# Smaller alternating loads, norm sums on VectorE and spread scaling, in place of interleaved filter rows, in a spectral mixer on one core

## The chip, the cores and the metric

The kernel runs on one core of a Trainium2 chip. Its time is the device time in microseconds of one execution; the median of 3 runs is quoted, with lowest and highest. A profiled execution gives the span from the first to the last instruction, and the time of that execution is some 2 us longer than its span. Five engines work side by side and wait for each other by semaphores: TensorE (PE; its weight loads are listed as PEld), VectorE (DVE), ScalarE (ACT), GpSimd (POOL) and SyncE (SP), which here only issues transfers. Each engine works through its own instructions strictly in the order in which they were written.

## The reference

One input x of 2048 rows (S) by 512 columns (D), bf16, goes through two blocks with residuals:

```python
h  = x + irfft2( rfft2(layernorm(x)) * (w_r + 1j*w_i) )      # w_r, w_i: 2048 x 257
h2 = h + mixer(layernorm(h))

def mixer(x):                    # token mixing: along S, for each column d
    n = layernorm(x)
    u = gelu(einsum("sd,sf->df", n, w1) + b1)                # w1: 2048 x 1376
    y = einsum("df,fs->ds", u, w2) + b2                      # w2: 1376 x 2048
    return y.T
```

The layer norms are over D and have no scale or shift; the gelu is the tanh form.

## The kernel before

Row s of x is s = 16 p + i: partition p of 128, and i from 0 to 15. What has one i is called slice i here, 128 x 512; x and the result lie in SBUF as 16 such slices. Both Fourier transforms are matmuls with constant matrices, which are stored in the program and loaded (FP, EM and IF). The stages, by the names that the kernel's helpers give them:

- **ln1**: mean and variance of every slice, and from the variance the reciprocal root r. There are two ways: on VectorE a statistics instruction and an aggregate (L640, L642); or on ScalarE two passes with an accumulator, sum and sum of squares (L619), then two small POOL operations and one on VectorE (L631 to L635). The root is ScalarE's (L611), the reciprocal VectorE's (L613). The mean isn't subtracted from x here: it would change only frequency 0 of the transform along D, which is zero after a norm and which the kernel leaves out.
- **scaling** ("fs"): r is put not on x but on the transform matrix of the slice, FS = FP * r, 128 x 256 (L649), on VectorE or POOL.
- **f1**: the first part of the transform along S. For each slice four matmuls with 256 columns, two for each half b of the columns of x. Four slices make a quarter; a quarter and a half b fill two PSUM banks, which one instruction of ScalarE or VectorE evacuates into Y (128 x 1024).
- **f2**: the transform along D, in 16 units G of four matmuls with 256 columns and one evacuation of 128 x 512 into CS.
- **x** (u = 0 to 7): the rest of the transform along S, four matmuls with 512 columns from two units of f2 into two banks; then the *filter products* on VectorE, which read these banks, multiply them by the filter rows W (real part w = 0 and imaginary part w = 1) and write V (L701). These read PSUM directly, so both banks stay taken until the last product of this u.
- **g1** (u = 0 to 7): first part of the inverse, 16 matmuls with 128 columns from V, evacuated into PQ.
- **g2, g3** (slices): the rest of the inverse. Four matmuls with 256 columns, an evacuation into EO by ScalarE, three more matmuls, and a sum with x on VectorE, which gives h.
- **ln2**: the second norm of each slice of h, for which VectorE and ScalarE again share the sums; HH is h normed.
- **mm1, gelu, mm2**: the mixer's two products, 176 matmuls with 512 columns each, the gelu between them, and the final sum and store of each slice.

No order is written out by hand. Every instruction is handed to a builder class with its inputs and outputs, an engine, an assumed duration (`dur`) and a priority (`prio`). The method `schedule` then lists the instructions: of those whose inputs are there, the one that can start first by the assumed durations is next, priority decides among equals; a PSUM unit takes the banks that are free first, with a limit on how many units of a class may be open at once. The constant `LATENCY` is the assumed time from an engine's end to another's start, and a transfer's landing follows assumed rates. These numbers set the order and the banks and nothing else: the engines then wait by semaphores, in that order. Several readers of one unit's banks are chained, each waiting for the one before, also when both are on VectorE.

What the prediction's steps touch: the loads of x and FP, alternately on SP's and ScalarE's queue (X pieces of 2 or 4 slices, FP in two pieces); the list SUMS, by which slices 2, 3, 6, 7, 10, 11 and 15 have their sums on ScalarE; the choice of VectorE or POOL for each scaling; W, one tile in which the rows of both parts alternate, so that one product of 128 x 2048 serves u = 1 to 6 whole (u = 0 and u = 7 are cut into smaller ones); and the helpers `stage_f2`, `stage_x`, `stage_g1`, of which the last cuts the final evacuation (u = 7, par = 0) in two halves, one for ScalarE and one for VectorE.

Of the kernel before, what the change touches and what calls it, by code (L numbers as in the profile page):

```python
# [143 lines left out]
LATENCY = {"sp": 0.0, "pe": 230.0, "act": 130.0, "dve": 110.0, "pool": 80.0}  # L144
# [36 lines left out]
class Builder:  # L181
# [110 lines left out]
    def schedule(self):  # L292
# [12 lines left out]
        while len(order) < len(ops):  # L305
# [52 lines left out]
            if o.is_dma:  # L358
                eng_free[e] = st + 430.0
                x0 = max(st + 1300.0, dma_free)  # L360
                dma_free = x0 + o.bytes / (o.rate or (290.0 if x0 < 7000.0 else 400.0))
                o.finish = o.done = dma_free + 900.0
            else:
                o.done = st + (o.dur[e] if isinstance(o.dur, dict) else o.dur)
                o.finish = o.done + (LATENCY[e] if o.lat is None else o.lat)
                eng_free[e] = o.done
# [90 lines left out]
def memory_layout():  # L457
# [30 lines left out]
    add("W", [NP, NG, 2, 257], bf, rw)  # L488
    add("HH", [NP, NS2, D_LEN], bf, rw)
    rv = region(32768)  # L490
    add("V", [NP, NG, 2, 256], bf, rv)
# [26 lines left out]
def build_kernel(nc, A_x, A_w_r, A_w_i, B_w1, B_b1, B_w2, B_b2, out):  # L518
# [5 lines left out]
    K = Builder(nc, {"f1": 4, "f2": 2, "x": 2, "g1": 2, "g1t": 2, "g2": 2, "g3": 2, "mm1": 5, "mm1b": 6, "mm2": 8})  # L524
# [5 lines left out]
    W = T["W"]  # L530
# [20 lines left out]
    DUR = {"act": {256: 310.0, 512: 520.0, 1024: 960.0}, "dve": {256: 350.0, 512: 640.0, 1024: 1150.0}}  # L551

    def evac(name, engine, dst, srcf, unit, n, prio, last=True, outs=None):
        def emit(s, eng, bank):
            if s == "act":
                return eng.activation(dst, srcf(bank), ACT.Copy)  # L556
            return eng.tensor_copy(dst, srcf(bank))  # L557
        return K.op(name, engine, emit, outs=outs or [dst], dur=DUR[engine][n], unit=unit, pr=True, last=last, prio=prio)

# [4 lines left out]
    K.op("half", "pool", lambda s, eng, bank: eng.memset(T["mh"][:, 0:1], -0.5), outs=[T["mh"][:, 0:1]], dur=100.0, prio=20)  # L564
# [8 lines left out]
    ld_x(0, 2)  # L573
    ld_x(2, 4, "act")
    ld_x(4, 8)
    ld_fp(0, 8, "act")
    ld_x(8, 12)
    ld_x(12, 16, "act")
    ld_fp(8, 16)
    dma("ld_EM", EM[:], cin["EM"][:, :], 6656 * 128, outs=[EM[:]], prio=29)  # L580

    for g0, g1 in ((0, 4), (4, 16), (16, 32)):
        h0 = max(g0, 1)
        for w, dram in ((0, A_w_r), (1, A_w_i)):
            for comp in range(2):
                dma(f"ld_w{w}p{comp}_{g0}", W[comp:NP:4, g0:g1, w, :], bass.AP(dram.tensor, g0 * 257, [[64 * 257, 32], [257, g1 - g0], [1, 257]]),
                    32 * (g1 - g0) * 514, outs=[W[comp:NP:4, g0:g1, w, 0:240]], prio=28, rate=290.0)
                p0 = 2 + comp
                if g0 == 0:
                    dma(f"ld_w{w}z{comp}", W[p0:NP:4, 0:1, w, :], bass.AP(dram.tensor, 32 * 257, [[64 * 257, 32], [257, 1], [1, 257]]), 32 * 514,  # L590
                        outs=[W[p0:NP:4, 0:1, w, 0:240]], prio=28)
                dma(f"ld_w{w}m{comp}_{g0}", W[p0:NP:4, h0:g1, w, :],
                    bass.AP(dram.tensor, (64 - h0) * 257, [[64 * 257, 32], [-257, g1 - h0], [1, 257]]),
                    32 * (g1 - h0) * 514, outs=[W[p0:NP:4, h0:g1, w, 0:240]], prio=28, rate=290.0)
# [10 lines left out]

    mv, rs, sd = T["mv1"], T["rs1"], T["sd1"]
# [9 lines left out]
    def sums_act(name, src, func, bias, acc, k, prio):  # L616
# [3 lines left out]
             ins=[src] + ([bias] if bias is not None else []), outs=[jk, acc], dur=620.0, lat=320.0, prio=prio)  # L620

    SUMS = (2, 3, 6, 7, 10, 11, 15)
    for i0, i1 in ((0, 2), (2, 4), (4, 6), (6, 8), (8, 10), (10, 12), (12, 14), (14, 15), (15, 16)):
        sl = slice(i0, i1)
        sx, sq = T["sx1"][:, sl], T["sq1"][:, sl]
        mean, var, nb = mv[:, sl, 0], mv[:, sl, 1], T["nb1"][:, sl]
        if i0 in SUMS:
# [9 lines left out]
        else:  # L637
            for i in range(i0, i1):
                st = T["st1"][:, i, 0:6]
                K.op(f"ln1_st{i}", "dve", lambda s, eng, bank, st=st, i=i: eng.bn_stats(st, X[:, i, :]), ins=[X[:, i, :]], outs=[st],  # L640
                     dur=600.0, prio=20)
                K.op(f"ln1_ag{i}", "dve", lambda s, eng, bank, st=st, i=i: eng.bn_aggr(mv[:, i, :], st), ins=[st], outs=[mv[:, i, :]],  # L642
                     dur=110.0, prio=23)
        rstd(1, sl, var, EPS[:, 0:1], 1.0, 25)
        for i in range(i0, i1):
            r = rs[:, i:i + 1]
            eng_ = "pool" if i < 12 and i % 2 == 0 else "dve"
            K.op(f"fs{i}", eng_,
                 lambda s, eng, bank, i=i, r=r: eng.tensor_scalar(FS[:, i, :, :], FP[:, i, :, :], r, None, op0=ALU.mult),  # L649
                 ins=[FP[:, i, :, :], r], outs=[FS[:, i, :, :]], dur={"pool": 980.0, "dve": 210.0}[eng_], prio=26)  # L650
# [5 lines left out]
    for q in range(4):  # L656
        for b in range(2):
            unit = PsumUnit("f1", 2)
            for n in range(4):
                n2 = 4 * q + n  # L660
# [11 lines left out]
            def src(bank):  # L672
                v = ps[:, bank:bank + 2, :].rearrange("p b (h g k) -> p (b h) g k", h=2, k=4)
                return v.rearrange("p n g k -> p g n k")
            evac(f"f1_{q}_{b}_ev", "dve" if q >= 1 and b == 0 else "act", Yv[:, b, :, 4 * q:4 * q + 4, :], src, unit, 1024, 14)


    def stage_f2(G):
        for pars in ((0,), (1,)) if G == 0 else ((0, 1),):
            unit = PsumUnit("f2", 1)  # L680
            for par in pars:
                for b in range(2):
                    mm(f"f2_{G}_{par}{b}", lambda bank, par=par: ps[:, bank, par * 256:par * 256 + 256],
                       Y[:, b, par, 2 * G:2 * G + 2, :].rearrange("p g k -> p (g k)"), E[:, b, par, :],
                       unit, b == 0, b == 1, par == pars[0] and b == 0, 12 - 0.05 * G, 256)
            y = slice(pars[0], pars[-1] + 1)
            evac(f"f2_{G}_ev{pars[0]}", "dve" if pars[0] else "act", CS[:, G, :, :].rearrange("p c (y j) -> p y c j", y=2)[:, y],
                 lambda bank, y=y: ps[:, bank, :].rearrange("p (y c j) -> p y c j", y=2, c=2)[:, y], unit, 256 * len(pars), 10)


    def times_filter(name, unit, u, srcf, gs, last, ys=slice(0, 2), ws=slice(0, 2)):
        g0, gn, gk = gs
        gsl = slice(g0, g0 + (gn - 1) * gk + 1, gk)
        nw, ny = ws.stop - ws.start, ys.stop - ys.start

        def tt(s, eng, bank):
            src = srcf(bank)
            wv = W[:, gsl, ws, 1:257].rearrange("p g w (j y) -> p g w y j", y=2)[:, :, :, ys, :]
            ov = V[:, gsl, ws, :].rearrange("p g w (y j) -> p g w y j", y=2)[:, :, :, ys, :]
            src = bass.AP(src.tensor, src.offset, [list(src.ap[0]), [256, gn], [0, nw], [128, ny], [1, 128]])  # L700
            return eng.tensor_tensor(ov, src, wv, ALU.mult)  # L701
        K.op(name, "dve", tt, ins=[W[:, gsl, ws, 1:240]], outs=[V[:, gsl, ws, ys.start * 128:ys.stop * 128]],
             dur=gn * nw * ny * 128 / 0.96 + 75.0, unit=unit, pr=True, last=last, prio=11)

    def stage_x(u):
        if u == 0:
            for i in range(2):
                unit = PsumUnit("x", 1)
                for r in range(2):
                    for cs in range(2):  # L710
                        mm(f"x_{u}_{r}{cs}{i}", lambda bank, r=r: ps[:, bank, r * 256:r * 256 + 256],
                           M[:, 2 if i == 0 and r == 0 else r, cs, :], CS[:, i, cs, :], unit, r == 0 and cs == 0, cs == 1, r == 0 and cs == 0, 13, 256,
                           skip=True)
                for w in range(2):
                    times_filter(f"x_{u}_w{i}{w}", unit, u, lambda bank: ps[:, bank, :], (i, 2, 2), w == 1, ws=slice(w, w + 1))
            return
        unit = PsumUnit("x", 2)
        for r in range(2):
            for cs in range(2):
                mm(f"x_{u}_{r}{cs}", lambda bank, r=r: ps[:, bank + r, :], M[:, r, cs, :], CS[:, 2 * u:2 * u + 2, cs, :],  # L720
                   unit, cs == 0, cs == 1, r == 0 and cs == 0, 13, 512)
        gs = (4 * u, 4, 1)
        if u < 7:
            times_filter(f"x_{u}_w", unit, u, lambda bank: ps[:, bank, :], gs, True)
        else:
            times_filter(f"x_{u}_w1", unit, u, lambda bank: ps[:, bank, 128:256], gs, False, ys=slice(1, 2))
            for w in range(2):
                times_filter(f"x_{u}_w0{w}", unit, u, lambda bank: ps[:, bank, 0:128], gs, w == 1, ys=slice(0, 1), ws=slice(w, w + 1))


    def stage_g1(u):
        for par in (1, 0):
            split = u == 7 and par == 0
            for gs in ((0, 1), (2, 3)) if split else ((0, 1, 2, 3),):
                unit = PsumUnit("g1t" if split else "g1", 1, early=True)
                for w in range(2):
                    for gi in gs:
                        g = 4 * u + gi
                        mm(f"g1_{g}_{par}{w}", lambda bank, gi=gi: ps[:, bank, gi * NP:gi * NP + NP],
# [151 lines left out]
```

## Time and profile before

| | |
|---|---|
| median of 3 runs | 138.36 us (138.27 to 138.36) |
| profiled execution: span, time | 136.0 us, 138.27 us |
| TensorE matmuls busy | 120.6 us (89%), 747 recorded |
| VectorE busy | 79.2 us (58%), 165 |
| ScalarE busy | 64.6 us (47%), 141 |
| POOL busy | 18.0 us (13%), 49 |
| read from HBM, written | 20.54 MB, 2.10 MB |

The profile's page lists the busy time of each engine, the span in slices, the transfers, and the chain of work that ended last: from the last instruction back, at each step, to what released it. A share in this chain says more than a busy share: what isn't in the chain has slack. The matmuls' durations reach from a matmul's start to the modelled end of its pipeline, so consecutive ones overlap: a 128 x 512 one is listed with 379 ns, and 49 of them in a row take 10.74 us, 0.219 us each. VectorE's and ScalarE's neighbours can overlap a little too. In a group's line stand the operation, what it writes and reads, its count, busy time and mean duration, and the idle time before it with what ended that.

### The profile page before, as it was taken

To read this page: it belongs to the slowest core of one execution; us is meant where nothing else is said; L and a number is where in the kernel's file an instruction comes from. 1 tells how busy PE (TensorE), PEld (TensorE's weight loads), DVE (VectorE), ACT (ScalarE), POOL (GpSimd) and SP (SyncE) were. 2 spreads that over 40 slices of the span, in tenths; PEclk is the share of its full clock that TensorE was granted. 3 is DMA by queue.
4 is the path that set the end of the run, shared out by engine and by line. 5 is a ranking of instruction groups with operands and counts; after the bars stand their busy time and mean duration, and the time that the engine had idled before them with its cause. 6 is when DMAs were issued, how large, how long until landed. Compare 5 with 4: busy or idle time off the path is not lost.

```text
span 136.0 us, 2049 instructions
## 1 busy us (share of the span) xinstructions
PE 120.6 (89%) x747; PEld 77.5 (57%) x756; DVE 79.2 (58%) x165; ACT 64.6 (47%) x141; POOL 18.0 (13%) x49
## 2 busy tenths in 40 slices
PE   0029779999998999999999999999999999999990
PEld 0027558668887756664444444445666666666660
DVE  0489985899992899996002686644444242332422
ACT  3699986558888899872004964633200000000000
POOL 1066900000000007567000000000000000000000
PEclk9999999999999999999999999999999999999999
DMA  4999999999999999970000000000021211112111
GB/s 117 354 380 396 292 294 292 309 406 425 418 419 300 337 417 295 314 293 2 5 0 0 0 0 0 0 0 0 0 82 39 77 39 47 68 43 77 39 51 67
DMA packets 15929, 22.76 MB, mean 167 GB/s; under 512 B 2640, under 2 KB 12880, under 8 KB 15280
## 3 DMA queue, kind: packets, MB, share of 16 engines
q1 hardware_dynamic: 15488, 21.33, 46.7%
q10 hardware_dynamic: 432, 1.31, 2.8%
q8 instruction: 6, 0.10, 0.3%
q14 instruction: 3, 0.02, 0.1%
HBM read 20.54 MB, written 2.10 MB: 166 GB/s over the span
## 4 chain that ended last, share of the span: by engine, by line
PE 80%; ACT 11%; DMA 3%; DVE 3%; issue 1%
PE ps L548 80%; ACT JK L619 6%; DMA X<-in_A_x_dram 3%; ACT PQ L556 3%; ACT sd L611 1%; DVE st L640 1%; DVE Y L557 1%; ACT EO L556 1%; ACT Y L556 1%; DVE OUT L839 1%; DVE mv L642 0%
## 5 line engine op out<-in xcount | busy, mean ns | idle before, releaser
L548 PE MATMUL ps<-HH,W 128*128 128x512 bf16 (+1 forms) x171 | 39.0, 379 | 0.3
L548 PE MATMUL ps<-GT,W 128*128 128x512 bf16 (+1 forms) x172 | 38.0, 379 | 0.2
L548 PEld LDWEIGHTS ps<-GT,W 128*128 128x128 bf16 (+1 forms) x176 | 25.3, 144 | 12.8 <-issue 0.2
L548 PEld LDWEIGHTS ps<-HH,W 128*128 128x128 bf16 (+1 forms) x176 | 17.6, 100 | 18.8
L839 DVE SCALAR_TENSOR_TENSOR OUT<-ps,B2f,H 128x512 bf16<-128x512 f32 x16 | 12.0, 751 | 23.8 <-PE ps L548 23.8
L701 DVE TENSOR_TENSOR V<-ps,W 128x512 bf16<-128x512 f32 (+2 forms) x13 | 18.3, 1463 | 1.3 <-PE ps L548 1.2
L548 PE MATMUL ps<-FS,X 128*128 128x256 bf16 x64 | 9.5, 317 | 10.1 <-POOL FS L649 9.4
L823 ACT ACTIVATE U<-ps,B1f 128x512 bf16<-128x512 f32 (+1 forms) x11 | 7.2, 687 | 14.7 <-PE ps L548 14.7
L548 PEld LDWEIGHTS ps<-FS,X 128*128 128x128 bf16 x64 | 7.0, 114 | 12.3 <-POOL FS L649 9.7
L825 DVE TENSOR_TENSOR Q<-U 128x512 bf16<-128x512 bf16 (+1 forms) x11 | 4.5, 421 | 13.4 <-ACT U L823 13.4
L782 DVE TENSOR_TENSOR H<-ps,X 128x512 bf16<-128x512 f32 x16 | 10.4, 675 | 2.2 <-PE ps L548 2.2
L556 ACT ACTIVATE CS<-ps 128x512 bf16<-128x512 f32 (+1 forms) x16 | 8.5, 586 | 3.6 <-PE ps L548 3.6
L556 ACT ACTIVATE EO<-ps 128x512 bf16<-128x512 f32 x16 | 8.7, 593 | 2.1 <-PE ps L548 2.1
L548 PE MATMUL ps<-EM,PQ 128*128 128x256 bf16 x64 | 9.3, 273 | 0.5 <-ACT PQ L556 0.5
L548 PE MATMUL ps<-EM,Y 128*128 128x256 bf16 x64 | 8.6, 273 | 1.0 <-DVE Y L557 1.0
L548 PE MATMUL ps<-EO,IF 128*128 128x256 bf16 (+1 forms) x48 | 9.2, 308 | 0.2 <-ACT EO L556 0.2
L556 ACT ACTIVATE PQ<-ps 128x512 bf16<-128x512 f32 (+1 forms) x16 | 8.2, 605 | 2.1 <-PE ps L548 2.1
L619 ACT ACTIVATE JK<-X 128x512 bf16<-128x512 bf16 x14 | 8.6, 614 | 1.1 <-DMA X<-in_A_x_dram 1.1
L640 DVE BATCH_NORM_STATS2 st<-X 128x6 f32<-128x512 bf16 x9 | 5.8, 677 | 5.2 <-DMA X<-in_A_x_dram 5.1
L829 ACT ACTIVATE SG<-P 128x512 bf16<-128x512 bf16 (+1 forms) x11 | 6.6, 624 | 4.7 <-DVE P L828 4.7
L619 ACT ACTIVATE JK<-H,nb 128x512 bf16<-128x512 bf16 x11 | 7.9, 721 | 1.7 <-DVE H L782 1.6
L548 PE MATMUL ps<-CS,EM 128*128 128x512 bf16 (+1 forms) x36 | 8.3, 355 | 0.0
(44 smaller groups left out, 104.5 us busy)
## 6 DMA issues: line engine op xcount, KB each, us to landing
W<-in_B_w_dram SPq DMA_DIRECT2D x4, 1376.0 KB, 14.9
W<-in_B_w_dram SPq DMA_DIRECT2D x10, 512.0 KB, 9.0
out_dram<-OUT SPq DMA_DIRECT2D x16, 128.0 KB, 1.7
W<-in_A_w_r_dram SPq DMA_DIRECT2D x4, 257.0 KB, 5.7
W<-in_A_w_i_dram SPq DMA_DIRECT2D x4, 257.0 KB, 5.5
X<-in_A_x_dram SPq DMA_DIRECT2D x2, 512.0 KB, 7.2
IF<-c_IF SPq DMA_DIRECT2D x1, 1024.0 KB, 8.5
EM<-c_EM SPq DMA_DIRECT2D x1, 832.0 KB, 11.0
```

Source lines behind the costliest of these rows:

```text
L548: return eng.matmul(outf(bank), lhsT, rhs, start=start, stop=stop, **({"skip_group_check": True} if skip else {}))
L556: return eng.activation(dst, srcf(bank), ACT.Copy)
L557: return eng.tensor_copy(dst, srcf(bank))
L611: K.op(f"ln{which}_sd{sl.start}", "act", lambda s, eng, bank: eng.activation(sd[:, sl], src, ACT.Sqrt, bias=bias, scale=scale), ins=[src, ...
L619: K.op(name, "act", lambda s, eng, bank: eng.activation(jk, src, func, accum_out=acc, **kw), ins=[src] + ([bias] if bias is not None else ...
L640: K.op(f"ln1_st{i}", "dve", lambda s, eng, bank, st=st, i=i: eng.bn_stats(st, X[:, i, :]), ins=[X[:, i, :]], outs=[st], dur=600.0, prio=20)
L701: return eng.tensor_tensor(ov, src, wv, ALU.mult)
L782: K.op(f"h_{s2}", "dve", lambda s, eng, bank, xs=xs, hs=hs: eng.tensor_tensor(hs, ps[:, bank, :], xs, ALU.add), ins=[xs], outs=[hs], dur=6 ...
L823: K.op(f"gelu{t}_u", "act", lambda s, eng, bank, U=U, bia=bia, Mt=Mt: eng.activation(U, ps[0:Mt, bank, :], ACT.Identity, bias=bia, scale=1.0),
L825: K.op(f"gelu{t}_q", "dve", lambda s, eng, bank, U=U, Q=Q: eng.tensor_tensor(Q, U, U, ALU.mult), ins=[U], outs=[Q], dur=350.0, prio=5)
L829: K.op(f"gelu{t}_sg", "act", lambda s, eng, bank, P2=P2, SG=SG: eng.activation(SG, P2, ACT.Sigmoid, scale=2.0 * GELU_C), ins=[P2], outs=[S ...
L839: K.op(f"fin{s2}", "dve", lambda s, eng, bank, dst=dst, bia=bia, hs=hs: eng.scalar_tensor_tensor(dst, ps[:, bank, :], bia, hs, op0=ALU.add ...
```

## The change

It touches the loads, the first norm, and everything up to the end of g1:

- x is loaded in seven pieces (slices 0, 1, 2-3, 4-5, 6-8, 9-11, 12-15) in place of five, FP in three in place of two, alternating between the two queues.
- ScalarE's sums are left for slices 1, 4 and 9 alone; the other 13 have VectorE's statistics. The groups that share one root are cut anew. For the three slices on ScalarE the reciprocal root becomes POOL's: an addition and a power.
- The scalings go to POOL (0, 3, 5, 7, 8), ScalarE (1, 2, 6, 9, 10) and VectorE (4 and 11 to 15); before, POOL had the even ones below 12 and VectorE the rest.
- f1 has three quarters as before and two last parts of two slices each, with evacuations of 128 x 512; its units may start before all their inputs are there, and up to eight may be open. A list (EVE) names the evacuating engine.
- W becomes two tiles, Wr and Wi, with V in the matching layout; every u has two products of 128 x 1024, one for each part. The filter rows are loaded in groups of 8, 8 and 16 in place of 4, 12 and 16, and half of them as one contiguous run for each partition.
- The cuts of the first f2 unit, of the first and last filter transform and of the last g1 evacuation are gone: these are whole units. VectorE evacuates f2's units 1 and 3, and the last one of g1. g1 takes par 0 before par 1, and the second-norm stage's first two g2 units no longer start early.
- The builder's assumed latencies, durations and transfer rates are changed, which changes the order.

```diff
-LATENCY = {"sp": 0.0, "pe": 230.0, "act": 130.0, "dve": 110.0, "pool": 80.0}
+LATENCY = {"sp": 0.0, "pe": 230.0, "act": 190.0, "dve": 150.0, "pool": 80.0}
...
-    add("W", [NP, NG, 2, 257], bf, rw)
+    add("Wr", [NP, NG, 257], bf, rw)
+    add("Wi", [NP, NG, 257], bf, rw + 16448)
...
-    add("V", [NP, NG, 2, 256], bf, rv)
+    add("V", [NP, 2, NG, 256], bf, rv)
...
-    K = Builder(nc, {"f1": 4, "f2": 2, "x": 2, "g1": 2, "g1t": 2, "g2": 2, "g3": 2, "mm1": 5, "mm1b": 6, "mm2": 8})
+    K = Builder(nc, {"f1": 8, "f2": 2, "x": 2, "g1": 2, "g2": 2, "g3": 2, "mm1": 5, "mm1b": 6, "mm2": 8})
...
-    ld_x(0, 2)
-    ld_x(2, 4, "act")
-    ld_x(4, 8)
-    ld_fp(0, 8, "act")
-    ld_x(8, 12)
-    ld_x(12, 16, "act")
-    ld_fp(8, 16)
+    ld_x(0, 1)
+    ld_x(1, 2, "act")
+    ld_x(2, 4)
+    ld_x(4, 6, "act")
+    ld_fp(0, 4)
+    ld_x(6, 9, "act")
+    ld_x(9, 12)
+    ld_fp(4, 10, "act")
+    ld_x(12, 16)
+    ld_fp(10, 16)
...
-    for g0, g1 in ((0, 4), (4, 16), (16, 32)):
+    for g0, g1 in ((0, 8), (8, 16), (16, 32)):
...
+    GROUPS = ((0, 1, False), (1, 2, True), (2, 4, False), (4, 5, True), (5, 7, False), (7, 9, False), (9, 10, True), (10, 11, False), (11, 13, False), (13, 15, False), (15, 16, False))
+    FSE = ('pool', 'act', 'act', 'pool', 'dve', 'pool', 'act', 'pool', 'pool', 'act', 'act', 'dve', 'dve', 'dve', 'dve', 'dve')
+    EVE = ('act', 'act', 'act', 'act', 'dve', 'act', 'act', 'dve', 'dve', 'act')
...
-        rstd(1, sl, var, EPS[:, 0:1], 1.0, 25)
+        if on_act:
+            rs = T["rs1"][:, sl]
+            K.op(f"ln1_e{i0}", "pool", lambda s, eng, bank, var=var, rs=rs: eng.tensor_scalar(rs, var, LN_EPS, None, op0=ALU.add),
+                 ins=[var], outs=[rs], dur=200.0, prio=24)
+            K.op(f"ln1_p{i0}", "pool", lambda s, eng, bank, rs=rs, n=i1 - i0: eng.tensor_tensor(rs, rs, T["mh"][:, 0:n], ALU.pow),
+                 ins=[rs, T["mh"][:, 0:4]], outs=[rs], dur=560.0, prio=25)
+        else:
+            rstd(1, sl, var, EPS[:, 0:1], 1.0, 25)
...
-            eng_ = "pool" if i < 12 and i % 2 == 0 else "dve"
...
+            def scale_fp(s, eng, bank, fsv=fsv, fpv=fpv, r=r):
+                if s == "act":
+                    return eng.activation(fsv, fpv, ACT.Copy, scale=r)
+                return eng.tensor_scalar(fsv, fpv, r, None, op0=ALU.mult)
...
-    for q in range(4):
+    for q0, q1 in ((0, 4), (4, 8), (8, 12), (12, 14), (14, 16)):
         for b in range(2):
-            unit = PsumUnit("f1", 2)
...
+            unit = PsumUnit("f1", (q1 - q0) // 2, early=True)
...
-            evac(f"f1_{q}_{b}_ev", "dve" if q >= 1 and b == 0 else "act", Yv[:, b, :, 4 * q:4 * q + 4, :], src, unit, 1024, 14)
+            evac(f"f1_{q0}_{b}_ev", EVE[2 * (0, 4, 8, 12, 14).index(q0) + b], Yv[:, b, :, q0:q1, :], src, unit, 512 * nb, 14)
...
+        evac(f"f2_{G}_ev", "dve" if G in (1, 3) else "act", dst, lambda bank: ps[:, bank, :].rearrange("p (y c j) -> p y c j", y=2, c=2), unit, 512, 10)
...
+        for w in range(2):
+            def tt(s, eng, bank, w=w):
+                src = ps[:, bank:bank + 2, :].rearrange("p r (i y j) -> p (r i) y j", i=2, y=2)
+                wv = Wx[w][:, 4 * u:4 * u + 4, 1:257].rearrange("p g (j y) -> p g y j", y=2)
+                ov = V[:, w, 4 * u:4 * u + 4, :].rearrange("p g (y j) -> p g y j", y=2)
+                return eng.tensor_tensor(ov, src, wv, ALU.mult)
+            K.op(f"x_{u}_w{w}", "dve", tt, ins=[Wx[w][:, 4 * u:4 * u + 4, 1:240]], outs=[V[:, w, 4 * u:4 * u + 4, :]],
+                 dur=1150.0, unit=unit, pr=True, last=w == 1, prio=11)
...
-        unit = PsumUnit("g2", 1, early=s2 < 2)
+        unit = PsumUnit("g2", 1)
```

## The prediction

> **What bounds the kernel now.** I read the page first, then the chain of waits in order of time, then the timeline up to 50 us, then the groups with shapes kept apart. TensorE is busy for 120.6 of 136.0 us, and the chain says where it isn't:
>
> ```profile
> 6.41 0.77 ACT JK L619 x3
> 7.45 1.41 ACT JK L619 x5
> 10.27 2.02 ACT JK L619 x7
> 19.19 1.24 DVE Y L557
> 20.56 18.16 PE ps L548 x172
> 38.75 3.54 ACT PQ L556 x7
> 42.34 2.80 PE ps L548 x22
> 49.04 7.33 PE ps L548 x51
> ```
>
> Until 15 us the chain runs through the norm sums on ScalarE, then through the first transform (f1) and its last evacuation; the second one (f2) starts at 20.56. From 49.04 on it is TensorE alone, and from 42.34 to the last matmul (132.90) next to nothing is idle. So a microsecond won or lost before 42.34 arrives at the end. Between 20.56 and 42.34 two engines are full at once:
>
> ```profile
> 20.50:30.00 9.50, 9.44 (x77) 6.88 (x78) 7.58 (x8) 5.40 (x12) 0.00 (x0) 1.00 1.17 326
> 30.00:42.30 12.30, 11.84 (x155) 9.98 (x152) 11.54 (x8) 10.69 (x22) 0.00 (x0) 1.00 1.01 426
> ```
>
> (columns: stretch, length, busy PE, weight loads, DVE, ACT, POOL, clock, DMA share, GB/s). The DVE's part is the filter products:
>
> ```profile
> 22.50 2.48 DVE L701 TENSOR_TENSOR V<-ps,W 128x512 bf16<-128x512 f32 x4 [0.88 <-PE ps L548]
> 25.33 15.86 DVE L701 TENSOR_TENSOR V<-ps,W 128x2048 bf16<-128x2048 f32 x9 [0.34 <-PE ps L548]
> 41.88 0.42 DVE L557 CAST PQ<-ps 128x256 bf16<-128x256 f32 x1 [0.69 <-PE ps L548]
> ```
>
> From 22.50 to 41.19 the DVE waits 0.34 us in all, and 1.15 us after its last product the next stage (g2) starts. The prices:
>
> ```profile
> L701 DVE TENSOR_TENSOR V<-ps,W 128x2048 bf16<-128x2048 f32 x6 | 13.3, 2281 | 0.3 <-PE ps L548 0.3
> L701 DVE TENSOR_TENSOR V<-ps,W 128x1024 bf16<-128x1024 f32 x1 | 1.2, 1210 | 0.0
> L640 DVE BATCH_NORM_STATS2 st<-X 128x6 f32<-128x512 bf16 x9 | 5.8, 677 | 5.2 <-DMA X<-in_A_x_dram 5.1
> L557 DVE CAST Y<-ps 128x1024 bf16<-128x1024 f32 x3 | 3.6, 1212 | 0.6 <-PE ps L548 0.6
> ```
>
> **The change, part by part.** The order of the instructions is that of the built programs; the clock of the sum is the profiled execution: 136.0 us of span, 138.27 us of time, so 2.27 us lie around the span; the median of the runs is 138.36.
>
> *Loads.* By one-microsecond stretches 0.25 MB have moved at 3.0 us, 0.65 at 4.0, 1.04 at 5.0, 1.34 at 6.0, 2.03 at 8.0, 2.82 at 10.0 and 3.25 at 11.0, and the first two pieces (0.52 MB, reached at 3.7) land at 4.55 and 4.76, about 0.9 later. With both queues sharing equally, the new pieces land at: slices 0 and 1 of x at 4.0, slices 2 to 5 at 5.3, the first matrix piece at 6.8, slices 6 to 8 at 7.7, 9 to 11 at 9.1, 12 to 15 at 10.8. All but the first four are there before VectorE asks for them, so finer pieces buy half a microsecond at the start. The fourth load on ScalarE's queue (0.43 us) moves its table load back, which ends at about 3.9, just before slice 1 lands. SP's queue holds two loads more ahead of EM (0.43 us each), which moves behind the same 3.1 MB of x and matrix as before: 0. Filter rows: the first group is twice as large (1.05 MB), lies behind EM (landed 13.6) and needs 3.5 us at 0.30 MB/us: 17.2, wanted after 22; the last group lands by 28, wanted at 32. Hidden; without that cover the first product would wait. Here the rows' 377 to 434 GB/s between 8 and 11 us, in 512 KB pieces, are the price I use.
> The Trainium skill ("DMA: Bandwidth & Descriptors", section "Bandwidth") speaks against pieces this small: it wants 1 MiB for three quarters of the peak and gives 341 GB/s there. An estimate from that page's figure puts slices 12 to 15 at 11.2 us, still ahead of their use, so the sum would be the same by rule and by row.
>
> *Norm sums and scaling, up to f2.* ScalarE loses 8 of 14 sums (0.61 us each as they follow one another, 4.9 us) and gains five scalings (not in the trace; between 0.28, its 128x2 row, and 0.61, its 128x512 SBUF row; nearest is 128x256 from PSUM, 0.38 to 0.45; I take 0.4; three of them stand ahead of a root that VectorE waits for, so the ends are worth 0.6 at most). POOL has one scaling less and three additions and powers more (0.2 and 0.58). VectorE gains four statistics and becomes the queue that decides. In the trace its instructions overlap: two statistics take 1.29 together, so 0.60 each in the queue, aggregates 0.10, reciprocals 0.09, variances 0.10, scalings 0.20 to 0.31. After slice 2 lands (5.3) it has 12 x 0.60 + 12 x 0.10 + 8 x 0.09 + 3 x 0.10 + 6 x 0.25 = 10.9. Waits in the written order: for slices 6 to 8, 0.1; for the variance of slice 4, 0.35, because POOL does that mean product only after two scalings of 0.98 (6.8 to 7.9 and 8.9 to 9.9) with a power of 0.58 between; for the root of slices 13 and 14, 0.3, which ScalarE does after the first f1 evacuation of the second quarter; latencies 0.1. Scalings end at 17.1. Then three evacuations stand in VectorE's queue, 1.21 + 0.69 + 0.69 (128x512 between the rows 128x256, 0.42, and 128x1024, 1.21) less 0.1 of overlap: 19.6, f2 at **19.7** against 20.56: **-0.85**. Ends: no waits, 18.8; every duration end to end (0.68, 0.17, 0.15, 0.17, 0.32), 22.6. The trace overlaps wherever there is no wait, so I stay near the lower and keep 21.0 as a likely upper end.
>
> *Matmuls of f1.* In the trace the first ones take 421 ns and follow each other every 0.213 us until 13.1, 3.9 us after the first, and 272 ns every 0.108 us from then on. After the change they start at 8.0 with pauses for the scalings at 8.9 and 12; I take full speed from 13.3. That f1 may now hold all eight banks ends the stall of 0.67 at 15.9, but TensorE then waits for scalings instead: 0.
> The Trainium skill ("TensorE: Matmul & The Clock Gate", section "What's actually happening") wants about 3.4 us of sustained work: an estimate of 12.8 by that, if the pauses do no harm. Nothing waits for matmuls then, so the sum is the same.
>
> *f2 to the first product.* Before, 22.50 - 20.56 = 1.94. Now the f2 units are whole and the first filter transform takes two of them: 17 f2 matmuls stand before its end (1.84), then its own (4 x 0.108, 0.217, and the last to its end, 0.38), 2.87 in all; VectorE's two f2 evacuations (0.69 each, from f2 + 1.05 and + 2.03) are done by then. First product at f2 + 2.90: **+0.96**.
>
> *Products.* 13 instructions become 16 of 128x1024, 1.21 each. Unconnected neighbours overlap by 0.08 (starts 25.33, 27.53, 29.73: 2.20 for 2.28), so 1.13; where both parts of one unit follow each other the second waits for the first (38.52 to 39.77: 1.25). That is 11 x 1.13 + 4 x 1.25 + 1.21 = 18.6, as before (18.69), plus waits. By PE's order: 0.1 before u=2; 0.4 before u=4, whose banks u=2 frees and which stands behind an f2 unit waiting for the fourth PQ evacuation (ScalarE, 0.52 each, from f2 + 8.6); then the largest: u=5 takes the bank pair of u=4, and PE holds 34 g1 (0.0575), 13 f2 (0.108) and then u=5's own four matmuls (0.65 + 0.38 to the end of the last) behind u=4: f2 + 11.39 + 0.87 + 1.96 + 1.40 + 1.03 = 16.65, where VectorE was free at 14.8: 1.85. In all 21.0: **+2.3**. Ends: no wait at all, 18.6 (+0); with every product 1.25 after the one before, +3.6.
>
> *Tail.* After the last product 8 g1 matmuls (0.40 + 0.22) and a whole PQ evacuation of 0.69 instead of two matmuls and a half one: 1.4 against 1.15: **+0.25**. The order of g2 and g3 puts the first matmul of the large product 14 places earlier, before its norm (root, reciprocal, 0.41) is ready; later matmuls that would fill this stand behind it: between 0 and 0.8, I take **+0.2**. The other regrouping of g1 and V's layout have the same bytes and columns: 0.
>
> Sum: -0.85 + 0.96 + 2.3 + 0.25 + 0.2 = +2.9; span 138.9, time **141.1**.
>
> **Rivals.**
> 1. *Products without waits* (ScalarE and PE run ahead of my rows): +2.3 falls away, 138.8; with half of them 140. For it: TensorE's work in the stage, 21.3 us, would fit. Against: the bank pair of u=5 is freed by u=4's last product, whatever the speeds.
> 2. *Faster*: the queue of VectorE up to f2 empties early. VectorE is idle when the last slices land, and f2 follows them. It decides from f2 at 16.8 on (20.56 - 3.75). For it: ScalarE's chain, which the profile shows as the limit, is 4.9 us shorter. Against: with the last slices at 10.8, their four statistics (2.8 with the aggregates), five scalings (1.25) and the evacuations (2.5) make 17.4 without one earlier leftover, so the slices must land earlier as well. With f2 at 16.5: 137.9.
> 3. *The clock stays low in f1*: pauses keep matmuls at 0.213 apart. From the second quarter on 48 x 0.213 = 10.2 from 12.3, and 0.6 of evacuation: f2 at 23.1, +3.4 on my sum, 144.5. For it: the pauses. Against: at that spacing PE has no pauses left.
> 4. *The halves cancel*: rival 1 with f2 at 19.1 instead of 19.7; 138.3.
>
> **How the numbers follow.** My sum 66 in 100 (139.6 to 142.6 by the bounds of f2's start and of the waits); rival 1 14 (two thirds of it above 138.7), rival 3 or VectorE's queue without overlap 8, rival 2 9, rival 4 3. A measurement of this kernel can tell about 0.2%, 0.28 us. Slower takes the first three, 0.88; same 0.03; faster 0.09. The range, 139.2 to 143.0, leaves out rivals 2 and 4, the low part of 1 and most of 3.
>
> **What would show it.** Right: 13 statistics and 6 ScalarE sums; f2 starts near 19.7; the first product 2.9 after it; one gap of 1.5 to 2 us on the DVE, released by PE, between the tenth and eleventh product; g2 near 45; TensorE without gaps after 53. Wrong: f2 before 18.5 or after 21.5, no such gap, f1 matmuls at 421 ns beyond 14 us, a product that waits for a DMA of W, or gaps in TensorE later than 55 us.

## The result and the profile after

The changed kernel takes **142.77 us** (median of 4 runs, 142.26 to 145.07), the kernel before beside it 138.31 us (138.15 to 138.36): a ratio of **1.031**, with a 95% interval of 1.028 to 1.034. In some executions of kernels with the changed filter stage TensorE's clock falls to half for a few microseconds right after it, and the ratios leave most of these executions out, so a median can stand above its ratio. The profiled execution has a span of 141.0 us against 136.0 and a time of 142.92.

The chain of waits of the changed kernel, in order of time (start, duration, what):

```profile
1.64 6.98 DMA FP<-c_FP
...
8.71 0.95 POOL FS L673
...
13.24 0.95 POOL FS L673
14.19 0.19 POOL rs L660
14.38 0.92 POOL FS L673
15.29 0.53 POOL rs L662
15.82 0.94 POOL FS L673
...
21.22 5.41 PE ps L549 x46
...
29.95 2.07 ACT PQ L557 x4
...
32.07 5.90 PE ps L549 x62
...
37.99 1.24 DVE V L731
...
46.81 2.03 PE ps L549 x16
...
52.35 7.66 PE ps L549 x54
```

Before, ScalarE's norm sums led to f2 at 20.56, and g2 started at 42.34. Now the chain begins with the first piece of the transform matrix, 6.98 us on its way, and goes on through POOL, which has almost no pause from 8.71 to 16.76 (between 10.84 and 11.96 the chain itself runs over ScalarE, whose sums POOL's next step needs). f2 starts at 21.22, later than before and not earlier, and g2 at 46.81. The large products start at 52.35 instead of 49.04; from there on both kernels are TensorE alone.

VectorE's products in the timeline of the changed kernel (start, busy time, instructions, in brackets the wait and what ended it), with TensorE's four matmuls for u = 5, and two groups:

```profile
24.24 2.35 DVE L731 TENSOR_TENSOR V<-ps,Wr 128x1024 bf16<-128x1024 f32 x2 [0.28 <-PE ps L549]
...
33.90 1.23 DVE L731 TENSOR_TENSOR V<-ps,Wr 128x1024 bf16<-128x1024 f32 x1 [0.32 <-PE ps L549]
...
35.26 1.23 DVE L731 TENSOR_TENSOR V<-ps,Wi 128x1024 bf16<-128x1024 f32 x1
...
36.92 1.03 PE L549 MATMUL ps<-CS,EM 128*128 128x512 bf16 x4
...
37.99 1.23 DVE L731 TENSOR_TENSOR V<-ps,Wr 128x1024 bf16<-128x1024 f32 x1 [1.50 <-PE ps L549]
...
44.03 1.22 DVE L731 TENSOR_TENSOR V<-ps,Wi 128x1024 bf16<-128x1024 f32 x1
45.97 0.69 DVE L558 CAST PQ<-ps 128x512 bf16<-128x512 f32 x1 [0.71 <-PE ps L549]
```

```profile
L731 DVE TENSOR_TENSOR V<-ps,Wr 128x1024 bf16<-128x1024 f32 x8 | 9.6, 1220 | 2.2 <-PE ps L549 2.1
L654 DVE BATCH_NORM_STATS2 st<-X 128x6 f32<-128x512 bf16 x13 | 8.5, 674 | 5.8 <-DMA X<-in_A_x_dram 5.8
```

The products run from 24.24 to 45.25, 21.0 us instead of 18.69, with one wait of 1.50 us before the eleventh, the first of u = 5. The matmuls for u = 5 start at 36.92 without a wait, in a row of 62 that keeps TensorE busy from 32.07 to 37.97. TensorE, which before was busy for 9.44 of the first 9.50 us of this stage and 11.84 of the next 12.30, has gaps now:

```profile
20.50:30.00 9.50, 8.61 (x72) 5.93 (x72) 7.62 (x8) 4.61 (x9) 0.00 (x0) 1.00 1.01 322
30.00:46.00 16.00, 13.95 (x159) 10.27 (x156) 13.22 (x13) 11.40 (x22) 0.00 (x0) 1.00 0.94 367
```

The difference of the two spans, stage by stage:

| | before | after | difference |
|---|---|---|---|
| f2 starts | 20.56 | 21.22 | +0.66 |
| from there to the first product | 1.94 | 3.02 | +1.08 |
| first to last product | 18.69 | 21.01 | +2.32 |
| last product to g2 | 1.15 | 1.56 | +0.41 |
| g2 to the last matmul | 90.56 | 91.14 | +0.58 |
| sum | | | +5.05 (spans: +5.0) |

Not all of this arrives in the time: the time lies 2.27 us above the span before and 1.92 after, so the two profiled executions differ by 4.65 us, and the medians by 4.46.

### The profile page after: what moved, and what is told of

Its sections match the earlier page's. It is cut to its first block, busy times and chain, and to the rows that moved or that the text cites. A ratio compares the mean times of both kernels' runs of the same rounds, so it can differ in the third digit from the quotient of the medians.

```text
span 141.0 us, 2046 instructions
## 1 busy us (share of the span) xinstructions
PE 121.7 (86%) x745; PEld 76.6 (54%) x754; DVE 81.4 (58%) x171; ACT 63.1 (45%) x128; POOL 18.5 (13%) x52
## 4 chain that ended last, share of the span: by engine, by line
PE 74%; DVE 9%; DMA 5%; POOL 4%; ACT 4%; issue 2%; SPq 1%
PE ps L549 74%; DVE V L731 5%; DMA FP<-c_FP 5%; POOL FS L673 3%; ACT PQ L557 1%; DVE H L782 1%; ACT Y L557 1%; POOL rs L662 1%; SPq L544 1%; DVE OUT L839 1%; DVE PQ L558 1%; DVE Y L558 0%; DVE st L788 0%; POOL rs L660 0%; ACT JK L634 0%
## 5 line engine op out<-in xcount | busy, mean ns | idle before, releaser
L654 DVE BATCH_NORM_STATS2 st<-X 128x6 f32<-128x512 bf16 x13 | 8.5, 674 | 5.8 <-DMA X<-in_A_x_dram 5.8
L549 PE MATMUL ps<-EM,V 128*128 128x128 bf16 x128 | 9.9, 219 | 1.9 <-DVE V L731 1.9
L731 DVE TENSOR_TENSOR V<-ps,Wr 128x1024 bf16<-128x1024 f32 x8 | 9.6, 1220 | 2.2 <-PE ps L549 2.1
L549 PEld LDWEIGHTS ps<-EM,V 128*128 128x128 bf16 x128 | 8.0, 98 | 4.6 <-DVE V L731 2.3
L557 ACT ACTIVATE PQ<-ps 128x512 bf16<-128x512 f32 x15 | 8.3, 598 | 4.9 <-PE ps L549 4.8
L549 PE MATMUL ps<-EM,Y 128*128 128x256 bf16 x64 | 9.3, 273 | 1.0 <-DVE Y L558 0.7
L557 ACT ACTIVATE CS<-ps 128x512 bf16<-128x512 f32 x14 | 8.0, 604 | 4.4 <-PE ps L549 4.4
L731 DVE TENSOR_TENSOR V<-ps,Wi 128x1024 bf16<-128x1024 f32 x8 | 9.6, 1220 | 0.2
```

What stands on the lines that cost most here:

```text
L549: return eng.matmul(outf(bank), lhsT, rhs, start=start, stop=stop, **({"skip_group_check": True} if skip else {}))
```

## The experiments

In every one the order of instructions on each engine and the PSUM banks are written into the kernel, taken from the built programs of before and after, so that an edit moves nothing else. Line numbers are shifted by that: the products are L731 in the changed kernel and L716 to L774 below. "Front" is everything up to the end of f1, "middle" is f2 to g1. The time of the kernel before, on the same chips, was 138.25 to 138.34 us in all groups of runs.

### The two halves of the change

*front_alone*: the changed kernel with the filter rows, f2, x, g1 and the tail of before.

```diff
-    add("Wr", [NP, NG, 257], bf, rw)
-    add("Wi", [NP, NG, 257], bf, rw + 16448)
+    add("W", [NP, NG, 2, 257], bf, rw)
...
-        for w in range(2):
-            def tt(s, eng, bank, w=w):
+            times_filter(f"x_{u}_w", unit, u, lambda bank: ps[:, bank, :], gs, True)
```

> The changed kernel's front (loads, norm sums, scalings, f1) with the middle of before (interleaved filter rows, products of 128x2048, f2 to g1 and everything behind), each part in its own kernel's order. By the changed kernel's trace, where f2 starts at 21.2 instead of 20.6, the front alone should cost 0.7 us: 139.0. By the prediction's term (f2 at 19.7) it should gain 0.85: 137.4.

Measured: 138.57 us, ratio 1.001 (0.999 to 1.003). *middle_alone* is the opposite, loads and norm of before with the middle of the change.

> The front of before with the changed kernel's middle (two filter tiles, products of 128x1024, whole units, g2 order), each in its own order. If the middle's cost is a matter of its own order and sizes, it is the four later terms read from the changed kernel's trace: first product +1.1, products +2.3, tail +0.4, ramp into the large product +0.6, so 4.4 more than before: 142.7. If part of it comes from the late f2 start of the changed kernel, it is less, 141 or below.

Measured: 142.78 us, ratio 1.035 (1.030 to 1.040). The chains of waits of the first and of the second:

```profile
21.25 18.17 PE ps L563 x172
...
43.03 2.03 PE ps L563 x16
```

```profile
20.40 5.46 PE ps L564 x46
...
46.03 2.03 PE ps L564 x16
```

From f2 to g2 the middle of before takes 21.78 us whatever stands in front, and the changed one 25.63. The front alone starts f2 at 21.25, 0.7 us late, yet costs only 0.25 us of median time, with an interval that holds 1; the middle alone costs as much as the whole change.

### The load pieces

*old_loads*: the changed kernel with the pieces of before. *front_old_loads*: the same edit in front_alone.

```diff
-    ld_x(0, 1)
-    ld_x(1, 2, "act")
-    ld_x(2, 4)
-    ld_x(4, 6, "act")
-    ld_fp(0, 4)
...
+    ld_x(0, 2)
+    ld_x(2, 4, "act")
+    ld_x(4, 8)
+    ld_fp(0, 8, "act")
...
```

> The changed kernel with the load pieces of before (x in five pieces, FP in two, same queues as before), all other instructions, their order and their banks as in the changed kernel. Theory: f2 is late because the small pieces move slowly and land late (first FP piece 8.6, x slices 6 to 8 at 9.1). Then FP lands at 8.2 and slices 4 to 7 at 7.2, VectorE's seventh statistic starts near 7.8 instead of 9.1, f2 at 19.7 to 20.2, time 141.3 to 141.8. Rival: VectorE's own queue (13 statistics, 6 scalings, 3 evacuations) sets f2, whatever lands when: f2 stays near 21.2, 142.8.

> As the front alone with the middle of before, but with the load pieces of before. Theory (late pieces): f2 at 19.7 to 20.2, 0.4 to 0.9 us better than before, 137.5 to 137.9, and better than both kernels. Rival (VectorE's queue): as the front alone, 139.0.

Measured: old_loads 144.23 us (142.26 to 144.84), ratio 1.038 (1.031 to 1.046). Its time is scattered by the clock after the filter stage and decides nothing here; its profile has f2 at 20.45, 0.77 us earlier than in the changed kernel. front_old_loads 138.21 us, ratio 1.000 (0.999 to 1.001), f2 at 20.50. Both miss the theory's 19.7 to 20.2. POOL's first scaling starts at 8.00 in it, at 8.71 in the changed kernel. The landing scatters: in six profiles with the small pieces and this order of POOL's queue the first matrix piece lands between 8.31 and 9.16, and f2 starts between 20.89 and 22.16, always later than in these two. So the small pieces cost some 0.7 us of f2's start. In the time it is 0.36 us by the medians (138.57 less 138.21), which the two overlapping intervals do not make sure. Even without the small pieces the shift of the sums from ScalarE to VectorE wins nothing. What the transfers moved between 5 and 7 us, before and then after (stretch, length, busy time of PE, weight loads, DVE, ACT and POOL, clock, busy share of the DMA engines, GB/s):

```profile
5.00:6.00 1.00, 0.00 (x0) 0.00 (x0) 1.00 (x4) 1.00 (x4) 0.00 (x0) 1.00 0.93 307
6.00:7.00 1.00, 0.00 (x0) 0.00 (x0) 0.25 (x2) 0.97 (x5) 0.00 (x0) 1.00 1.04 320
```

```profile
5.00:6.00 1.00, 0.00 (x0) 0.00 (x0) 0.69 (x3) 1.00 (x4) 0.24 (x2) 1.00 1.02 242
6.00:7.00 1.00, 0.00 (x0) 0.00 (x0) 1.00 (x7) 0.43 (x3) 0.00 (x0) 1.00 0.86 206
```

The DMA engines are about as busy (1.02 and 0.86 against 0.93 and 1.04) and move a fifth and a third less.

*early_matrix*: front_alone with the first matrix piece as SP's second transfer, and x in the larger pieces of before.

```diff
-    ld_x(0, 1)
-    ld_x(1, 2, "act")
-    ld_x(2, 4)
-    ld_x(4, 6, "act")
-    ld_fp(0, 4)
...
+    ld_x(0, 2)
+    ld_x(2, 4, "act")
+    ld_fp(0, 4)
+    ld_x(4, 8, "act")
...
```

> The front of the changed kernel (sums on VectorE, scaling spread) with the filter order and tail of before, and the first quarter of the matrix issued as SP's second transfer, behind one piece of x of two slices. Theory (f2 is late because POOL's first scaling waits for the first matrix piece, which landed at 8.6 us in the changed kernel and at 8.0 with the old pieces): the piece now lands at 6.2 to 7.2, f2 starts at 19.2 to 19.9 instead of 20.5, and the time is 137.2 to 137.8, faster than both kernels. Rival (VectorE's own queue of statistics and the last x pieces set the start of f2, not the matrix): f2 stays at 20.4 or later and the time is 138.2 or more.

Measured: 137.90 us, ratio 0.997 (0.996 to 0.999). POOL's first scaling starts at 7.63, not at 6.2 to 7.2, and slices 4 to 7 of x land only at 8.19, where the chain of waits now begins; the profiled execution, the slowest of the twelve, has f2 at 21.2. A small gain in time, and a miss for the mechanism: in this profile what the matrix wins in the transfers, x loses.

### POOL's queue

Both kernels have the middle and the tail of before. *short_pool* starts from front_old_loads, *short_pool_new* from front_alone, with the small pieces. In the list fs is a scaling, e and p are the addition and the power that make a root, me and m2 the two steps of a mean product; the number is the slice.

```diff
  POOL:
-   fs0, ln1_e1, ln1_me4, ln1_p1, fs3, ln1_m24, ln1_me9, ln1_e4, ln1_m29, ln1_p4, fs5, ln1_e9, fs7, ln1_p9, fs8
+   ln1_e1, ln1_p1, ln1_me4, ln1_m24, fs0, ln1_e4, ln1_p4, fs3, ln1_me9, ln1_m29, fs5, ln1_e9, ln1_p9, fs7
  VectorE:
-   ..., ln1_st7, ln1_ag6, ln1_st8, ln1_ag7, ln1_va4, ..., ln1_ag13, ln1_st14
+   ..., ln1_va4, ln1_st7, ln1_ag6, ln1_st8, ln1_ag7, ..., ln1_ag13, fs8, ln1_st14
```

> The front of the changed kernel with the load pieces, the filter order and the tail of before, as in front_old_loads (138.21), and POOL's queue altered: the four small steps for slices 1 and 4 (inverse root, mean product) stand ahead of the first scaling, which waits for the first matrix piece, and the scaling of slice 8 goes to VectorE. Theory (behind the first matrix piece POOL's queue is the chain that sets f1: in front_old_loads it runs without a pause from 12.0 to 16.0 us): f2 starts at 19.7 to 20.0 instead of 20.5 and the time is 137.4 to 137.7, faster than both kernels. Rival (VectorE and the last pieces of x set f1 just as much): f2 at 20.3 or later, 138.1 or more.

> The same alteration of POOL's queue with the small load pieces of the change, to be held against front_alone (138.57). Theory (the late first matrix piece, 8.6 us, costs because POOL's small steps stand behind the scaling that waits for it): with these steps in front 0.7 to 0.9 us come back, f2 at 20.3 to 20.5, 137.7 to 137.9. Rival (the piece is late for the matmuls themselves, whatever the queue's order): 138.4 or more.

Measured: short_pool **137.63 us**, ratio 0.995 (0.993 to 0.996), f2 at 19.74. short_pool_new **137.41 us**, ratio 0.995 (0.993 to 0.997), f2 at 19.90. Both are 0.5% faster than the kernel before, with intervals clear of 1. POOL's timeline in the changed kernel and in short_pool_new:

```profile
8.71 0.95 POOL L673 TENSOR_SCALAR FS<-FP,rs 128x256 bf16<-128x256 bf16 x1 [3.39 <-DMA FP<-c_FP]
9.74 0.23 POOL L660 TENSOR_SCALAR rs<-mv 128x1 f32<-128x1 f32 x1
10.05 0.22 POOL L645 TENSOR_SCALAR mv<-sx 128x1 f32<-128x1 f32 x1
...
15.81 0.94 POOL L673 TENSOR_SCALAR FS<-FP,rs 128x256 bf16<-128x256 bf16 x1
```

```profile
6.98 0.57 POOL L669 TENSOR_TENSOR rs<-rs,mh 128x1 f32<-128x1 f32 x1
7.63 0.23 POOL L652 TENSOR_SCALAR mv<-sx 128x1 f32<-128x1 f32 x1
...
8.30 0.95 POOL L680 TENSOR_SCALAR FS<-FP,rs 128x256 bf16<-128x256 bf16 x1 [0.16 <-DMA FP<-c_FP]
...
13.64 0.94 POOL L680 TENSOR_SCALAR FS<-FP,rs 128x256 bf16<-128x256 bf16 x1
```

Against front_alone the same small pieces win 1.16 us by the medians (138.57 less 137.41) and 0.9 by the ratios, more than expected. In the changed kernel POOL waits 3.39 us for the matrix with steps ready behind the waiting scaling; done in that time, and with one scaling of 0.94 us less, its last scaling starts 2.2 us earlier. The piece itself also landed some 0.4 us earlier in this profile, which is a part of it; in old_tail, which has the front of the changed kernel, it landed at 8.31, about as early, and f2 started at 20.89 and not at 19.90. The two edits, the order and the scaling that goes to VectorE, were not tried apart.

With POOL's queue short another one leads. The chain of short_pool starts with a piece of x and runs through VectorE's statistics before it comes to POOL's last scaling:

```profile
1.63 8.25 DMA X<-in_A_x_dram
...
9.90 0.69 DVE st L658
...
13.68 0.94 POOL FS L677
```

### The products

*split_products*: the kernel before with the six products of 128 x 2048 cut in two.

```diff
-            times_filter(f"x_{u}_w", unit, u, lambda bank: ps[:, bank, :], gs, True)
+            for w in range(2):
+                times_filter(f"x_{u}_w{w}", unit, u, lambda bank: ps[:, bank, :], gs, w == 1, ws=slice(w, w + 1))
```

> The kernel before with each VectorE product of 128x2048 for u = 1 to 6 split into two neighbours of 128x1024; nothing else is moved. Theory (products go one behind the other on VectorE and set the stage): by the measured 1.25 and 1.13 against 2.20 us, 6 times 0.18, so +1.1 us and 139.4. Rival (the split is hidden, since the first half can start earlier): 138.3.

Measured: 139.59 us, ratio 1.0086 (1.0065 to 1.0107), +1.34 us against 138.25. The timeline:

```profile
25.66 17.20 DVE L716 TENSOR_TENSOR V<-ps,W 128x1024 bf16<-128x1024 f32 x15 [0.73 <-PE ps L563]
```

Nine instructions took 15.86 us before; these fifteen take 17.20, 0.22 more for each cut. The cut is paid in full here.

*early_u5*: the changed kernel; the filter transform for u = 5 gets other banks and stands ahead of g1 of u = 4, so that it no longer waits for u = 4's last product.

```diff
  TensorE:
-   x_4, g1_2 (rest), g1_3, f2_10, f2_11, g1_4 (w = 0), f2_12, f2_13, g1_4 (most of w = 1), x_5 (banks of x_4)
+   x_4, f2_10, f2_11, g1_2 (rest), g1_3, g1_4 (par 0, w = 0), x_5 (banks 2 and 3), g1_4 (par 1, w = 0), f2_12, f2_13, g1_4 (w = 1)
```

> The changed kernel with the filter transform for u = 5 given other banks and put ahead of the last g1 matmuls of u = 4, so that it no longer waits for u = 4's last product to free its banks; the last block of f2 is moved ahead of it. Theory (VectorE's 1.5 us of waiting between the tenth and the eleventh product is this wait for the banks): the gap goes, 1.4 to 1.6 us less, 141.2. Rival (TensorE's or ScalarE's work in this stretch is the bound, and the wait comes back at another product): 142.8.

Measured: 143.30 us, ratio 1.034 (1.031 to 1.036): nothing is won. The waits in VectorE's timeline:

```profile
38.04 1.23 DVE L746 TENSOR_TENSOR V<-ps,Wr 128x1024 bf16<-128x1024 f32 x1 [0.62 <-PE ps L564]
...
41.58 1.23 DVE L746 TENSOR_TENSOR V<-ps,Wr 128x1024 bf16<-128x1024 f32 x1 [1.05 <-PE ps L564]
```

The 1.50 has become 0.62 and 1.05, before u = 5 and u = 6 (the clock of this profile is 1.00 up to 44 us). TensorE's matmuls for these two now wait 0.37 and 0.30 us for evacuations of ScalarE. So the rival holds: the banks were not what u = 5 waited for.

*half_first*: the changed kernel with the first filter transform as before, f2's first unit in two halves and u = 0 in two units of one bank. ScalarE evacuates f2's units 1 and 3 again, as before.

```diff
+        if G == 0:
+            for par in range(2):
+                unit = PsumUnit("f2", 1)
...
+        if u == 0:
+            for i in range(2):
+                unit = PsumUnit("x", 1)
...
```

> The changed kernel with the first filter transform as before: the first f2 unit in two halves, u = 0 in two units of two groups with four products of 128x512. Theory (the terms of the sum add: the first product waits 1.08 us longer behind f2 than before the change): the first product comes 1.9 to 2.0 us after f2 instead of 3.0, and the time is 141.6 to 142.0. Rival (TensorE's and ScalarE's order in the products sets the stage, and the time won at its head is lost again as waits of VectorE): 142.6 or more, with over 2.3 us of waits between the products.

Measured: 143.36 us, ratio 1.036 (1.035 to 1.038). In the timeline the first product comes 1.93 us after f2 (21.19), and the time is lost again (the clock is 1.00 up to 44 us in this profile too):

```profile
23.12 1.29 DVE L756 TENSOR_TENSOR V<-ps,Wr 128x512 bf16<-128x512 f32 x2 [0.88 <-PE ps L564]
...
29.43 2.36 DVE L774 TENSOR_TENSOR V<-ps,Wr 128x1024 bf16<-128x1024 f32 x2 [1.21 <-PE ps L564]
...
38.45 1.23 DVE L774 TENSOR_TENSOR V<-ps,Wr 128x1024 bf16<-128x1024 f32 x1 [1.50 <-PE ps L564]
```

Here TensorE has g1 of u = 0 and three f2 units in front of the transform for u = 2.

*steady_order*: half_first with the order and the banks of f2, x and g1 rewritten, the products unchanged (u = 1 to 7 have fourteen; the sixteen below counts u = 0 uncut).

```diff
  TensorE, for u = 2 to 7 (f2 in banks 6 and 7, g1 in 0 and 1, x_u in 4 and 5 or 2 and 3 by turns):
+   f2_(2u+2), x_u, f2_(2u+3), g1_(u-2) par 0, g1_(u-2) par 1
  then:
+   g1_6, g1_7
```

> The changed kernel with the same sixteen whole products for u = 1 to 7, the first filter transform as in half_first, and only the order and the banks of f2, the filter transforms and g1 rewritten: f2 runs one unit ahead of each filter transform, the bank pairs of the transforms alternate so that u never waits for u - 1, and g1 follows two units behind. Theory (beyond the cost of the split, some 1.3 us as in split_products, it is the order of TensorE's queue and the banks that stretch the products): waits between the products under 0.8 us in all, g2 23.2 to 23.9 us after f2 instead of 25.6, and the time is 140.4 to 141.3. Rival (ScalarE's evacuations or the split products themselves set the stage, whatever TensorE's order): 142.3 or more.

Measured: **141.08 us**, ratio 1.019 (1.017 to 1.020). The chain of waits and, in the second fence, the only wait inside the products and the tail:

```profile
21.57 2.80 PE ps L563 x24
...
26.88 14.70 PE ps L563 x152
...
45.52 2.04 PE ps L563 x16
```

```profile
33.80 1.22 DVE L773 TENSOR_TENSOR V<-ps,Wr 128x1024 bf16<-128x1024 f32 x1 [0.24 <-PE ps L563]
...
44.77 0.69 DVE L572 CAST PQ<-ps 128x512 bf16<-128x512 f32 x1 [0.94 <-PE ps L563]
```

TensorE runs 14.70 us on end, and f2 to g2 takes 23.95 us instead of 25.59. So the order and the banks, with the first transform as before, account for 1.7 us of the time (142.77 less 141.08); the first transform alone had won nothing. What is left of the middle, 2.17 us over before's 21.78, is 1.64 in the products (20.33 from first to last against 18.69; 1.34 is the measured price of the cuts) and 0.53 in the tail.

### The tail

*old_tail*: the changed kernel with the order of g2, g3, ln2 and mm1 of before (and the order of before for the loads of w2).

```diff
  TensorE:
-   ..., g2_4, g2_5, g3_3, mm1 (2 matmuls), g2_6, mm1 (1), g3_4, mm1 (1), g2_7, mm1 (1), g3_5, g2_8, ...
+   ..., g2_4, g3_3, g2_5, g2_6, g3_4, g2_7, g3_5, mm1 (3 matmuls), g2_8, mm1 (1), ...
```

> The changed kernel with the order of the g2, g3, ln2 and mm1 instructions of before; front and filter products as in the changed kernel. Theory (the way from the last product to the first matmul of mm1 is 0.6 us longer since the change): 142.2, that is 0.4 to 0.6 below the changed kernel. Rival (the ramp is set by the last products and the evacuation halves, not by the order after them): 142.8, as the changed kernel.

Measured: 143.03 us as a median, ratio 1.026 (1.023 to 1.028) against the changed kernel's 1.031. With the clock up it is 141.97 (three runs), the changed kernel 142.62 (three runs): 0.65 less, though the intervals of the two ratios touch. The profile says the same: from g2's start to the end of the span before took 93.66 us (136.0 less 42.34), the changed kernel 94.19, this one 93.53 (140.0 less 46.47). The order after the products had cost the half microsecond. The expectation names the wrong stretch: from the last product to the first matmul of mm1 the changed kernel takes 7.10 us and the kernel before 7.85, so this matmul comes earlier. But it then holds up TensorE, as it waits for its norm:

```profile
52.35 0.38 PE L549 MATMUL ps<-HH,W 128*128 128x512 bf16 x1 [0.81 <-DVE HH L802]
```

In old_tail the first three matmuls of mm1 start at 52.93, behind other work and without a wait.

## Why the prediction was right, and where it wasn't

The sign and the range held. The size came out short: +2.9 us of span forecast, +5.0 in the profile. 142.77 lies near the upper end of 139.2 to 143.0 and just above the bounds of the prediction's own sum, 139.6 to 142.6. Term by term:

- **f2's start, forecast -0.85, measured +0.66.** This is the step that failed, with 1.5 of the 2.1 us missed. It failed first in "the first matrix piece at 6.8": that used the rates of before's pieces for the smaller ones, and the piece landed at 8.6 (slices 6 to 8: 9.1, not 7.7). The very first pieces were right: VectorE takes slices at 3.79 and 5.31, against 4.0 and 5.3. It failed second in "VectorE becomes the queue that decides": the chain shows POOL, from the moment the matrix lands. I had counted a wait of 0.35 us for POOL's mean product behind two scalings, the first of them at 6.8; that scaling started at 8.71, after a wait of 3.39 us with ready steps behind it. From the landing to f2 it is 12.6 us in five profiles with this front (8.31 to 20.89, 8.60 to 21.19, 8.62 to 21.22, 8.66 to 21.25, 8.98 to 21.57; in early_u5 9.16 to 22.16), so here the landing sets f2. front_old_loads shows that with the larger pieces f2 still stands at 20.50; short_pool and short_pool_new show that a shorter queue with no waiting scaling ahead of ready steps gives the 19.7 to 19.9 which I had forecast, and in short_pool the chain does run through VectorE's statistics. The page of the Trainium skill that I weighed here, "DMA: Bandwidth & Descriptors" (section "Bandwidth"), asks for large transfers; I held that the sum is the same by rule and row. The rows spoke for the rule: 242 and 206 GB/s against 307 and 320 between 5 and 7 us, the same direction; how much of this is the transfers' size and how much their place in the two queues was not told apart.
- **f2 to the first product, forecast +0.96, measured +1.08.** Right as a stretch, but not a term of its own: half_first takes it away and wins nothing, because the transform for u = 2 still stands behind g1 and f2 and VectorE waits 1.21 us there.
- **Products, forecast +2.3, measured +2.32, with the wait of 1.85 at 1.50 and where I had put it.** The size was right, in part by luck: the waits inside the stretch were 1.82 us (0.32 and 1.50) against 2.35 forecast, and the products without them took 19.19 against 18.6. The sum of TensorE's queue that put the eleventh product at f2 + 16.65 was right as well: it came at f2 + 16.77. But the banks, which rival 1 was turned down with, were not the reason: u = 4's last product ended at 36.49, and the matmuls for u = 5 followed at 36.92 in an unbroken row of TensorE's. early_u5 takes other banks, and the wait comes back in two others. The runs show two costs. The cut products are 1.3 us (split_products), more than I had for them: I took 18.6 us for the sixteen without waits, and steady_order's products take 20.33 with 0.24 of waiting for TensorE. The order of TensorE's queue and the banks over the whole stage, head and products together, are 1.7 us (steady_order).
- **Tail, forecast +0.25, measured +0.41; the order of g2 and g3, forecast +0.2, measured +0.58 (from g2 to the last matmul).** The mechanism was right: the first matmul of the large product waits 0.81 us for its norm. The size was too small, in the second within the 0 to 0.8 given; old_tail returns the second.
- **The clock in f1 (rival 3)** did not stay low, nor did rivals 1, 2 and 4 come about. Rival 2 has the part of the truth that the front can be made faster, but through POOL's order, and by about 1 us, not by 3.75.

A sum of single terms fitted the whole only because each term was a measured stretch of the same chain. The terms of the middle could not be taken out one at a time.

## What to carry to other kernels

On an in-order engine, look at what stands behind an instruction that waits for a transfer: moving ready steps ahead of it, together with one scaling moved to another engine, took a front that had been no faster than before to 0.5% faster. Where two engines are full in one stage, removing the one wait that shows can just move it, as in early_u5 and half_first; what won time was a new order for the whole stage. Rates read from the large transfers of one kernel were not the price of the same bytes in smaller pieces and another order of the queues.

## What the runs showed of the hardware

**TensorE's clock fell behind a half-idle stage, without any long pause.** In the profiled execution of old_loads thirteen g2 matmuls of 256 columns take 2.93 us; the same thirteen take 1.58 us in the changed kernel:

```profile
46.27 2.93 PE L564 MATMUL ps<-EM,PQ 128*128 128x256 bf16 x13 [0.88 <-DVE PQ L573]
```

```profile
46.81 1.58 PE L549 MATMUL ps<-EM,PQ 128*128 128x256 bf16 x13 [0.88 <-DVE PQ L558]
```

In half_first the windows show the fall behind the stretch in which TensorE waits for the last products (columns as above; the clock is the third figure from the end):

```profile
44.00:48.00 4.00, 1.96 (x21) 1.39 (x21) 2.37 (x3) 1.50 (x3) 0.00 (x0) 0.77 1.02 351
48.00:52.00 4.00, 4.00 (x18) 2.48 (x17) 0.69 (x1) 1.86 (x4) 0.00 (x0) 0.50 1.03 413
```

TensorE was busy for half of 44 to 48 us and then ran at half clock although it had no gap. In old_loads no single wait of TensorE in this stretch was longer than 0.9 us. The page "TensorE: Matmul & The Clock Gate" of the Trainium skill (section "What's actually happening") ties the low clock to an idle window of about 3.4 us; here it fell behind a window with work in half of it. The share of work alone does not decide it: between 44 and 48 us TensorE was busy for 2.58 of 4 us in old_loads, at a clock of 0.60, and for 2.42 in the changed kernel's profile, at 1.00. The kernels with the filter order of before, whose TensorE is full in this stage, showed no clock below 0.996 in any execution. That the gaps cause the fall was not tried by itself.

**Scaling 128 x 256 in SBUF** takes ScalarE 0.51 us (forecast 0.4), POOL 0.95 and VectorE 0.23 in a row of two or three.
